# Attention and two gated MLPs on one core: more places for loaded rows, full-height factor matmuls, and a last chunk finished block by block

## The chip, the cores and the metric

One core of one Trainium2 chip runs the whole program. The metric is the device time of one execution in microseconds. Times of the kernel before are from three timed runs, and one more execution was taken by the profiler.

## The reference

```python
# attention: 4 batches, 8 heads, 576 positions, head width 64; scale = 1/8
scores = scale * q @ k.T                                   # causal
cum    = cumsum(max(s, 0))
scores = where(causal, -1e9, scores + min(-(cum_i - cum_j), 0))
attn   = softmax(scores);  x = attn @ v                    # as 2304 tokens x 512
# layer 1: RMS norm, then a gated MLP, 512 -> 1536 -> 512
xn = x / sqrt(mean(x*x) + 1e-6) * rms_g
x1 = (silu(xn @ w_gate) * (xn @ w_val)) @ w_out
# layer 2: the same without the norm
y  = (silu(x1 @ w2_gate) * (x1 @ w2_val)) @ w2_out
```

## The kernel before

Every large product is made of three float32r matmuls: an operand is split into a rounded part (H) and its rest (L), and H*H, H*L and L*H are summed. ACT rounds, DVE or POOL subtracts to get the rest. The engines' instruction order is written by a planner at build time: `Plan.op` records each operation with a cost in ns, what it reads and writes, and a priority; `Plan.run` lists them engine by engine, always the ready one of smallest priority number. A changed cost, buffer or dependency can therefore move any instruction behind it. The SP queue, which issues nearly all DMAs, runs in order: a load whose buffer is not yet free holds back everything behind it.

The program has five stretches. **Attention with the first layer's gate and value products** (0 to 442 us): the heads of one batch are worked on while the matmuls of the batch before (`gate_value`, L1116) fill TensorE's free places. After each batch `normalise` makes the norm's factors: per token and head one number, which a transpose brings into the first 16 partitions of a tile (`rT`, L1089); a matmul with the constant matrix `sel` (L1096) spreads these 16 rows over 128 partitions, four such matmuls a batch, and the result scales x. `sel` has 16 partitions, so this matmul uses 16 of TensorE's 128 rows. `rT` lies in the place of xH's last quarter, which is overwritten with rounded x afterwards. **The rest of those products** (442 to 506). **The first output stage** (506 to 626): two passes of `strassen_out`, each of seven products of a block with 512 tokens (Strassen's scheme), and a `plain_out` over the last 256 tokens. **Layer 2's gate and value products** (626 to about 896), which store rows to DRAM. **The second output stage** (from about 896): the same two kinds of passes, then the stores of the result.

In an output stage a row of the hidden layer (128 x 512, or x 256 in `plain_out`) comes in by `fetch_row`: a load by SP into a place of ring "h" (L1453), the rounding by ACT into ring "H" (L1395), the rest by DVE into ring "L" (L1398). A row serves six matmuls of `strassen_out` (L1478), or twelve of `plain_out` (L1533). Each of the three rings has four places, used in turn: a load waits until the row four back has been subtracted from, and a rounding until TensorE is through with the row four back. At a product's end ACT copies the two banks out (`keep`, L1488) or DVE adds them (`add`, L1494). `sums_of_rows` (L1178 loads, L1183, L1186 stores) prepares sums of rows for the second pass beside the first pass, on the same SP queue and on DVE.

At the very end, `plain_out` goes through the twelve rows, and within a row through the four output blocks (dd). `store_rest` copies each block out in two halves, 128 columns by DVE with a store on SP, 128 by ACT with a store on ACT's queue.

Of the kernel before, what the change touches and what calls it, by code (L numbers as in the profile page):

```python
# [333 lines left out]
def tile_kernel(  # L334
# [80 lines left out]
    sel = buf("m1", "sel", [2 * NH, 2 * KD, D], F32R)  # L415
# [106 lines left out]
    def setup():  # L522
# [17 lines left out]
        for x in (xs, xL[0], *xH):  # L540
            op(NONE, 0, lambda en, x=x: x.bufs[0](), w=[])
        op(ACT, 450, lambda en: en.dma_start(out=cum(), in_=s), w=[cum], pri=-3e6, later=2000)
# [37 lines left out]
        def later():  # L580
            def selectors(en):
                for j in range(2):
                    en.memset(half()[64 * j:64 * j + 64, j:j + 1], 1.0)
                    en.memset(half()[64 * j:64 * j + 64, 1 - j:2 - j], 0.0)
                en.memset(f32(zsel()), 0.0)
                for j in range(2):
                    en.memset(f32(zsel()[64 * j:64 * j + 64, 2 * KD - 2 + j:2 * KD - 1 + j]), 1.0)
                en.tensor_tensor(
                    out=sel()[:],
# [5 lines left out]
            op([(POOL, 1800), (DVE, 1200)], 0, selectors, r=[ident, "early 1"], w=[half, zsel, sel], pri=5.5)  # L595
# [367 lines left out]
    def normalise(H, L, g, tot, pri, split=True):  # L963
# [93 lines left out]
        def rT():  # L1057
            return H(KD - 1, lo, n)[:2 * NH]
# [30 lines left out]
        op(ACT, c_act(n), lambda en: en.activation(rT(), tp()[:2 * NH, skip:skip + n], ACTF.Copy),  # L1089
           r=[tp], w=last, pri=pri)  # L1090
        banks = (ps, mo_bank())
        for k in range(KD):
# [3 lines left out]
            op(PE, (c_mm(n) + 90, 2 * NH), lambda en, rs=rs, k=k: en.matmul(  # L1096
# [427 lines left out]
    def plain_out(row, WO, ring, acc, tiles, pri, scale=1.0, store=None):  # L1524

        n = 256
        for f in range(KF):
            H, L = fetch_row(ring, *row(f), n, pri + f)
            for dd in range(KD):
                name = "A11 A21 A12 A22".split()[dd // 2 + 2 * (f // K6)]  # L1530
                for i, (z, xx) in enumerate(((0, H), (0, L), (1, H))):
                    part, w = weight(WO, name, f % K6, dd % 2, z)
                    op(PE, c_mm(n), lambda en, dd=dd, w=w, xx=xx, f=f, i=i: en.matmul(  # L1533
                        acc[dd]()[:, :n], w(), xx(), start=f == 0 and i == 0,
                        stop=f == KF - 1 and i == 2), r=[part, xx],
                       w=[acc[dd]] if f or dd or i else acc, pri=pri + f)
# [216 lines left out]
    extra = {z: two(free_w[i], F32 if z == "h" else F32R, "h" + z) for i, z in enumerate("hHL")}  # L1753
# [180 lines left out]
```

## Time and profile before

| what | us |
|---|---|
| median of 3 runs | 1046.23 |
| lowest and highest | 1043.33, 1046.81 |
| profiled execution, its own time | 1044.21 |
| its span, first to last instruction | 1042.4 |
| PE busy | 1031.7 (99%) |
| DVE, ACT, POOL busy | 769.5 (74%), 633.9 (61%), 261.2 (25%) |
| DMA | 212.07 MB, mean 203 GB/s |

PE is TensorE's matmuls, DVE is VectorE, ACT is ScalarE, POOL is GpSimd; "SPq" and "ACTq" are the queues that issue DMAs. Matmuls are pipelined and overlap in the records, so the time that one takes is the distance from its start to the next start, not its recorded duration, and a PE that shows as busy can still be slower than its best. The granted clock is TensorE's, as a share of 2.4 GHz; 1.00 is the upper of its two levels.

### The profile page before, as it was taken

To read this page: it belongs to the slowest core of one execution; us is meant where nothing else is said; L and a number is where in the kernel's file an instruction comes from. 1 tells how busy PE (TensorE), PEld (TensorE's weight loads), DVE (VectorE), ACT (ScalarE), POOL (GpSimd) and SP (SyncE) were. 2 spreads that over 40 slices of the span, in tenths; PEclk is the share of its full clock that TensorE was granted. 3 is DMA by queue.
4 is the path that set the end of the run, shared out by engine and by line. 5 is a ranking of instruction groups with operands and counts; after the bars stand their busy time and mean duration, and the time that the engine had idled before them with its cause. 6 is when DMAs were issued, how large, how long until landed. Compare 5 with 4: busy or idle time off the path is not lost.

```text
span 1042.4 us, 17573 instructions
## 1 busy us (share of the span) xinstructions
PE 1031.7 (99%) x5546; PEld 901.1 (86%) x5546; DVE 769.5 (74%) x1751; ACT 633.9 (61%) x1318; POOL 261.2 (25%) x351
## 2 busy tenths in 40 slices
PE   9999999999999999999999999999999999999998
PEld 9988888998999899899887889888888888878888
DVE  7989877778778787568878987766668667876562
ACT  6889877766676465234466866455665455665652
POOL 3668744443333240100000000211222221300000
PEclk9999999999999999999999999999999999999999
DMA  9874533433345674378887662676676767888673
GB/s 326 267 244 136 185 123 110 132 116 121 99 138 151 220 241 155 124 236 264 279 282 250 199 207 96 223 236 207 213 239 220 249 239 245 281 273 252 217 241 99
DMA packets 123293, 212.07 MB, mean 203 GB/s; under 512 B 19072, under 2 KB 47488, under 8 KB 123200
## 3 DMA queue, kind: packets, MB, share of 16 engines
q1 hardware_dynamic: 122576, 210.61, 62.3%
q8 instruction: 44, 0.72, 0.3%
q10 hardware_dynamic: 624, 0.34, 0.1%
q14 instruction: 49, 0.40, 0.1%
HBM read 146.33 MB, written 64.56 MB: 202 GB/s over the span
## 4 chain that ended last, share of the span: by engine, by line
PE 88%; DMA 5%; DVE 3%; ACT 2%; issue 1%; SPq 0%; POOL 0%; ACTq 0%; DVEq 0%; POOLq 0%
PE mo L1116 24%; PE mo L1649 11%; PE sps L1649 9%; PE mo L1478 7%; PE tp L1478 6%; PE tp L787 5%; PE sps L1478 4%; PE tp L775 3%; PE sps L705 3%; PE mo L1725 3%; PE mo L1533 2%; PE tp L1649 1%; PE sps L1116 1%; PE tp L1116 1%; DMA h_d<-t 1%; PE sps L830 1%
## 5 line engine op out<-in xcount | busy, mean ns | idle before, releaser
L1398 DVE TENSOR_TENSOR hL<-hh,hH 128x512 fp32r<-128x512 f32 (+1 forms) x192 | 126.5, 667 | 70.4 <-ACT hH L1395 69.5
L1116 PE MATMUL mo<-xH,L 128*128 128x448 f32 (+2 forms) x472 | 171.8, 364 | 0.2 <-DVE L L488 0.2
L1116 PE MATMUL mo<-xL,H 128*128 128x448 f32 (+2 forms) x472 | 170.9, 362 | 0.6 <-DVE xL L1105 0.6
L1116 PE MATMUL mo<-xH,H 128*128 128x448 f32 (+2 forms) x472 | 170.5, 362 | 0.0
L1395 ACT ACTIVATE hH<-hh 128x512 fp32r<-128x512 f32 (+1 forms) x192 | 114.9, 603 | 89.8 <-DVE hL L1398 21.3
L1478 PE MATMUL mo<-hH,wo 128*128 128x512 f32 x312 | 98.3, 390 | 0.4 <-ACT hH L1395 0.4
L1116 PEld LDWEIGHTS mo<-xL,H 128*128 128x128 f32 x472 | 88.8, 188 | 8.2 <-issue 1.2
L1116 PEld LDWEIGHTS mo<-xH,L 128*128 128x128 f32 x472 | 88.8, 188 | 7.8 <-issue 1.2
L1116 PEld LDWEIGHTS mo<-xH,H 128*128 128x128 f32 x472 | 88.8, 188 | 6.2 <-issue 0.2
L742 ACT ACTIVATE sc<-sc,col 128x256 f32<-128x256 f32 (+2 forms) x96 | 60.6, 631 | 48.0 <-DVE col L731 47.6
L1478 PEld LDWEIGHTS mo<-hH,wo 128*128 128x128 f32 x312 | 58.6, 188 | 13.2 <-ACT hH L1395 1.2
L780 DVE TENSOR_TENSOR pTB<-tp,pTB 128x512 fp32r<-128x512 f32 (+1 forms) x96 | 56.3, 596 | 12.4 <-ACT pTB L778 11.9
L1655 ACT ACTIVATE u<-sps 128x512 f32<-128x512 f32 x48 | 28.6, 595 | 55.0 <-PE sps L1649 53.1
L1478 PE MATMUL mo<-hL,wo 128*128 128x512 f32 x156 | 61.3, 393 | 0.7 <-DVE hL L1398 0.4
L1478 PE MATMUL tp<-hH,wo 128*128 128x512 f32 x192 | 60.4, 389 | 0.0
L778 ACT ACTIVATE pTB<-tp 128x512 fp32r<-128x512 f32 (+1 forms) x96 | 48.8, 519 | 18.5 <-PE tp L775 17.7
L787 PEld LDWEIGHTS tp<-pTB,vst 128*128 128x128 f32 x320 | 52.9, 188 | 4.0 <-DVE pTB L780 0.3
L787 PE MATMUL tp<-pTB,vst 128*128 128x448 f32 (+3 forms) x320 | 55.3, 314 | 0.0
L1478 PE MATMUL sps<-hH,wo 128*128 128x512 f32 x168 | 53.2, 390 | 0.2 <-ACT hH L1395 0.2
L775 PE MATMUL tp<-ident,sc 128*128 128x128 f32 x320 | 51.3, 273 | 1.4 <-ACT sc L742 1.3
L719 POOL TENSOR_SCALAR_AFFINE_SELECT sc<-cb 128x128 f32<-128x128 f32 x96 | 34.6, 375 | 54.8 <-PE tp L775 48.0
L1664 ACT ACTIVATE u<-u 128x512 f32<-128x512 f32 x48 | 29.7, 631 | 30.0 <-DVE u L1659 29.9
(291 smaller groups left out, 2783.1 us busy)
## 6 DMA issues: line engine op xcount, KB each, us to landing
raw<-in_w_gv SPq DMA_DIRECT2D x44, 511.8 KB, 5.8
tb<-h_d SPq DMA_DIRECT2D x48, 256.0 KB, 3.6
t<-tb SPq DMA_DIRECT2D x48, 256.0 KB, 2.6
hh<-t SPq DMA_DIRECT2D x48, 256.0 KB, 3.3
lq<-in_qk SPq DMA_DIRECT2D x32, 288.0 KB, 4.0
cb<-cum_d SPq DMA_DIRECT2D x32, 288.0 KB, 3.6
hh<-h_d SPq DMA_DIRECT2D x36, 256.0 KB, 3.6
row0B<-u SPq DMA_DIRECT2D x24, 256.0 KB, 3.5
```

What stands on the lines that cost most here:

```text
L705: op(PE, c_mm(n), lambda en, pt=pt, at=at, c=c, n=n, z=z, kk=kk: en.matmul(pt()[:, :n], qst[j]()[:, at:at + 128], kk()[:, c:c + n], start= ...
L719: op(POOL, 165 + 0.85 * m, lambda en: en.affine_select(out=sc()[:m, o:o + m], in_=cb()[:m, o:o + m], pattern=[[-1, m]], base=0, compare_op ...
L742: op(ACT, c_act(o + m, 2) + 35, lambda en: en.activation(sc()[:m, :o + m], sc()[:m, :o + m], ACTF.Exp, scale=-1.0, bias=col()[:m, 0, t:t + 1],
L775: op(PE, C_TR, lambda en, pt=pt, a=a, kb=kb, t=t: en.transpose(pt()[:, a * P:a * P + P], self.sc[t]()[:, kb * P:kb * P + P], ident()), r=[ ...
L778: op(ACT, c_act(n), lambda en, pt=pt, c=c: en.activation(place(H, c), source(pt, c), ACTF.Copy), r=[pt], w=[(H, c)], pri=pri)
L780: op(DVE, c_tt(n), lambda en, pt=pt, c=c: en.tensor_tensor(out=place(L, c), in0=source(pt, c), in1=f32(place(H, c)), op=ALU.subtract), r=[ ...
L787: op(PE, c_mm(n), lambda en, w=w, z=z, kb=kb, d0=d0, n=n, o=o: en.matmul(po()[:, o:o + n], vst[j]()[:, kb, :], pT[z]()[:, d0:d0 + n], star ...
L1116: op(PE, c_mm(n), lambda en, a=a, x=x, c=c, k=k, i=i: en.matmul(ps()[:, :n], a()[:, c], x(k, lo, n), start=(k == 0 and i == 0), stop=(k == ...
L1395: op(ACT, c_act(n) + 35, lambda en: en.activation(H(), src(), ACTF.Copy), r=[src, *after], w=[H], pri=pri)
L1398: lambda en: en.tensor_tensor(out=L(), in0=src(), in1=f32(H()), op=ALU.subtract),
L1478: op(PE, c_mm(n), lambda en, m=m, w=w, xx=xx, kk=kk, i=i: en.matmul(ps[m]()[:, :n], w(), xx(), start=first and kk == 0 and i == 0, stop=kk ...
L1649: op(PE, c_mm(n), lambda en, w=w, xx=xx, cut=cut, kk=kk, i=i: en.matmul(ps()[:, :n], W[w]()[:, cut], xx(), start=first and kk == 0 and i == 0,
```

## The change

Three things. `sel` gets 128 partitions, zero below the first 16, and the factor matmul reads all 128 rows of `rT`'s place; for that the last quarter of both xH buffers is set to zero once at the start, and the set-up of the constants waits for DVE's `cumulate` by an instruction that reads its result. In both output stages ring "h" gets six places, rings "H" and "L" three. The last `plain_out` goes through its last two rows block by block, and `store_rest` copies each block out whole, in turn by DVE (with SP's queue) and ACT (with its own).

```diff
-    sel = buf("m1", "sel", [2 * NH, 2 * KD, D], F32R)
+    sel = buf("m1", "sel", [P, 2 * KD, D], F32R)
...
+        for x, n in zip(xH, (512, NQ)):
+            op([(POOL, 520), (DVE, 400)], 0, lambda en, x=x, n=n: en.memset(
+                f32(x(KD - 1, 0, n)), 0.0), w=x.keys(KD - 1, ALL), pri=4.5)
...
             def selectors(en):
+                en.tensor_scalar(out=fenced()[:, 1:2], in0=f32(cumHL()[:, :1]), scalar1=1.0,
+                                 scalar2=1.0, op0=ALU.mult, op1=ALU.mult)
...
+                en.memset(f32(sel()), 0.0)
                 en.tensor_tensor(
-                    out=sel()[:],
+                    out=sel()[:2 * NH],
...
-            op([(POOL, 1800), (DVE, 1200)], 0, selectors, r=[ident, "early 1"], w=[half, zsel, sel], pri=5.5)
+            op([(POOL, 2300), (DVE, 1500)], 0, selectors, r=[ident, cumHL, "early 1"],
+               w=[half, zsel, sel], pri=5.5)
...
         def rT():
-            return H(KD - 1, lo, n)[:2 * NH]
+            return H(KD - 1, lo, n)
...
-            op(PE, (c_mm(n) + 90, 2 * NH), lambda en, rs=rs, k=k: en.matmul(
+            op(PE, c_mm(n) + 90 * (not split), lambda en, rs=rs, k=k: en.matmul(
                 rs(), sel()[:, 2 * k:2 * k + 2].rearrange("p h d -> p (h d)"),
                 rT(),
                 start=True, stop=True), r=[sel, *last], w=[rs], pri=pri)
...
-    def plain_out(row, WO, ring, acc, tiles, pri, scale=1.0, store=None):
+    def plain_out(row, WO, ring, acc, tiles, pri, scale=1.0, store=None, tail=0):
...
+        ends = []
         for f in range(KF):
             H, L = fetch_row(ring, *row(f), n, pri + f)
+            if f >= KF - tail:
+                ends.append((f, H, L))
+                continue
             for dd in range(KD):
...
+                products(dd, f, H, L, pri + f)
+        for dd in range(KD):
+            for end in ends:
+                products(dd, *end, pri + KF + dd)
...
+    extra = [two(free_w[i], F32R if i == 2 else F32, "hr"[i == 2]) for i in range(3)]
...
+            + single(f"h{z}1", F32 if z == "h" else F32R, "h" + z) for z in "hHL"}
+    ring["h"] += extra[0] + extra[1]
+    ring["H"].append(extra[2][0])
+    ring["L"].append(extra[2][1])
...
+    last_r = two(free_w[20], F32R, "hr")
+    ring = {"h": [x for t in ("hh0", "hh1", "tmp0", "tmp1") for x in single(t, F32, "hh")]
+            + two(free_w[19], F32, "hh"),
+            "H": [x for t in ("hH0", "hH1") for x in single(t, F32R, "hH")] + last_r[:1],
+            "L": [x for t in ("hL0", "hL1") for x in single(t, F32R, "hL")] + last_r[1:]}
...
     def store_rest(xo, ps, dd):
-        for z, e in enumerate((DVE, ACT)):
...
+        if dd % 2:
+            op(ACT, c_act(256), lambda en: en.activation(xo(), ps()[:, :256], ACTF.Copy), r=[ps],
+               w=[xo], pri=-1.0e4)
+        else:
+            op(DVE, c_tt(256), lambda en: en.tensor_copy(xo(), ps()[:, :256]), r=[ps], w=[xo],
+               pri=-1.0e4)
+        op((SP, ACT)[dd % 2], (4 * P * 256, 450)[dd % 2], lambda en: en.dma_start(
+            out=outT[dd * P:(dd + 1) * P, 2048:2304], in_=xo()),
+           r=[xo], w=[("out4", dd)], pri=-1.0e4)
```

Three places show how the written order moves. First SP's queue, in the middle of the first pass of `strassen_out`: `hh` and `h` are places of the ring of loaded rows, `h_d` and `t` rows and sums of rows in DRAM, `tb` the buffers of `sums_of_rows`. The kernel before:

```order
L1186 DMA t_85<-tb 128x512
L1453 DMA hh<-t_83 128x512 x4
L1186 DMA t_87<-tb 128x512
L1453 DMA hh<-t_83 128x512
L1186 DMA t_86<-tb 128x512
L1453 DMA hh<-t_83 128x512
L1186 DMA t_88<-tb 128x512
L1453 DMA hh<-h_d_70 128x512 x6
```

and the changed one at the same place:

```order
L1461 DMA hh<-t_83 128x512 x2
L1194 DMA t_85<-tb 128x512
L1461 DMA h<-t_83 128x512 x4
L1194 DMA t_87<-tb 128x512
L1461 DMA hh<-h_d_70 128x512
L1194 DMA t_86<-tb 128x512
L1461 DMA hh<-h_d_70 128x512
L1461 DMA h<-h_d_70 128x512 x4
L1194 DMA t_88<-tb 128x512
```

The loads stand further ahead of the stores of the sums: before, the six loads of `h_d_70` come behind all four stores, now the first comes ahead of the third store and the other five ahead of the fourth.

Second ACT's order at the start of the same pass, where `hH` and `r` are places of the ring of rounded rows and `x` the copies of a finished product (`keep`). Before:

```order
L1395 ACTIVATE hH<-hh 128x512 x5
L1488 ACTIVATE x_6396<-sps_6326 128x512
L1488 ACTIVATE x_6396<-sps_6332 128x512
L1395 ACTIVATE hH<-hh 128x512 x6
L1488 ACTIVATE x_6396<-tp_6401 128x512
L1488 ACTIVATE x_6396<-tp_6408 128x512
```

and in the changed kernel:

```order
L1403 ACTIVATE r<-h 128x512
L1403 ACTIVATE wo<-ov 128x512
...
L1403 ACTIVATE hH<-h 128x512 x2
L1403 ACTIVATE r<-h 128x512
L1403 ACTIVATE hH<-hh 128x512 x2
L1496 ACTIVATE x_6399<-sps_6329 128x512
L1496 ACTIVATE x_6399<-sps_6335 128x512
L1403 ACTIVATE r<-h 128x512
L1403 ACTIVATE hH<-h 128x512 x2
```

Before the first pair of copies nine rows are rounded in the kernel before (four of them further up) and eight in the changed one (three further up), so that the rounding runs three rows ahead of a product's end before, and two now; between two pairs of copies there are six roundings in both.

Third the end of PE's queue, where `mo0` to `mo3` are the banks of the four output blocks, `hH`, `hL` the parts of a row, and `hr` the third place, which holds both parts. Before, the last row (each line of two other such lines for the rest left out):

```order
L1533 MATMUL mo0_10632<-hH_9697,wo_9807 128x256
L1533 MATMUL mo0_10632<-hL_9705,wo_9807 128x256
...
L1533 MATMUL mo2_10638<-hH_9697,wo_9807 128x256
...
L1533 MATMUL mo1_10643<-hH_9697,wo_9773 128x256
...
L1533 MATMUL mo3_10648<-hH_9697,wo_9773 128x256
```

and in the changed kernel the last two rows:

```order
L1540 MATMUL mo2_10635<-hr_9700,wo_9810 128x256 x3
L1540 MATMUL mo0_10641<-hH_8848,wo_9810 128x256
...
L1540 MATMUL mo0_10641<-hr_9700,wo_9810 128x256 x3
...
L1540 MATMUL mo3_10646<-hr_9700,wo_9775 128x256 x3
...
L1540 MATMUL mo1_10651<-hr_9700,wo_9775 128x256 x3
```

Before, a block gets its last three matmuls three apart, all within the last twelve; now a block is finished with six matmuls in a row, and the four blocks end six matmuls apart.

## Rows read from the trace of the kernel before

**Rows 1.** Windows by stage: busy us (x instructions) by engine, granted clock, DMA share.

```profile
60.00:442.00 382.00, 380.41 (x2192) 341.43 (x2190) 296.39 (x906) 257.70 (x607) 164.38 (x244) 1.00 0.47 149
...
506.00:575.00 69.00, 67.43 (x290) 53.68 (x289) 53.15 (x87) 42.08 (x73) 1.58 (x1) 1.00 0.84 267
575.00:626.00 51.00, 51.00 (x233) 42.28 (x232) 45.92 (x78) 36.87 (x68) 1.30 (x1) 1.00 0.66 205
```

**Rows 2.** One line, L1096, the factor matmuls: durations in ns, first and last start.

```profile
L1096 PE MATMUL mo<-xH,sel x24: 275/462/470, 30.7 to 441.6; 16*128 16x448 f32 x16, 16*128 16x256 f32 x8
```

**Rows 3.** Timeline, PE, around one factor matmul: start us, us, instruction.

```profile
339.85 0.37 PE L1116 MATMUL mo<-xH,H 128*128 128x448 f32 x1
340.05 0.37 PE L1116 MATMUL mo<-xL,H 128*128 128x448 f32 x1
340.35 0.46 PE L1096 MATMUL mo<-xH,sel 16*128 16x448 f32 x1
340.74 0.47 PE L1116 MATMUL mo<-xH,L 128*128 128x448 f32 x1
341.05 0.37 PE L1116 MATMUL mo<-xH,H 128*128 128x448 f32 x1
```

**Rows 4.** Timeline, PE, around two factor matmuls in a row.

```profile
336.94 0.37 PE L1116 MATMUL mo<-xH,H 128*128 128x448 f32 x1
337.23 0.67 PE L1096 MATMUL mo<-xH,sel 16*128 16x448 f32 x2
337.84 0.47 PE L1116 MATMUL mo<-xL,H 128*128 128x448 f32 x1
```

**Rows 5.** Chain that ended last, first output stage: start us, us, what.

```profile
506.10 8.18 PE sps L1478 x36
...
565.07 5.25 DMA hh<-h_d
...
575.09 8.18 PE tp L1478 x36
```

**Rows 6.** Timeline, ACT, two idle stretches of that stage.

```profile
546.42 1.94 ACT L1395 ACTIVATE hH<-hh 128x512 fp32r<-128x512 f32 x3 [1.96 <-DMA hh<-h_d]
...
557.21 0.63 ACT L1395 ACTIVATE xHB<-x 128x512 fp32r<-128x512 f32 x1 [2.76 <-DVE x L1494]
```

**Rows 7.** Timeline, ACT, then DVE, at the end of one product.

```profile
513.69 1.22 ACT L1488 ACTIVATE x<-sps 128x512 f32<-128x512 f32 x2
...
515.46 0.69 DVE L1398 TENSOR_TENSOR hL<-hh,hH 128x512 fp32r<-128x512 f32 x1 [0.55 <-ACT hH L1395]
...
518.31 0.68 DVE L1183 TENSOR_TENSOR tb<-tb 128x512 f32<-128x512 f32 x1
```

**Rows 8.** Timeline, PE, start of the second output stage.

```profile
919.09 0.83 PE L1478 MATMUL mo<-hH,wo 128*128 128x512 f32 x2
920.15 0.50 PE L1478 MATMUL mo<-hL,wo 128*128 128x512 f32 x1 [0.23 <-DVE hL L1398]
```

**Rows 9.** Timeline, all engines, end of the program.

```profile
1037.48 1.37 DVE L1865 COPY oo<-mo 128x128 f32<-128x128 f32 x4 [3.81 <-PE mo L1533]
...
1038.24 0.28 PE L1533 MATMUL mo<-hH,wo 128*128 128x256 f32 x1
...
1040.04 0.34 ACTq L1868 DMA_DIRECT2D out_dram<-oo  x1
```

**Rows 10.** DMA issues of the last 27 us: KB each, median us to landing.

```profile
hh<-rest_d SPq DMA_DIRECT2D x11, 128.0 KB, 2.1
...
out_dram<-oo ACTq DMA_DIRECT2D x4, 64.0 KB, 1.7
```

**Rows 11.** DMA issues, whole program: stores of 128 KB.

```profile
h_d<-t SPq DMA_DIRECT2D x22, 128.0 KB, 3.4
```

**Rows 12.** One line, L959, a copy of 256 columns by ACT.

```profile
L959 ACT ACTIVATE x<-mo x5: 383/383/384, 16.8 to 36.1; 128x256 f32<-128x256 f32 x5
```

**Rows 13.** Timeline, POOL, first instruction after the set-up.

```profile
20.79 0.81 POOL L485 TENSOR_SCALAR H<-raw 128x512 fp32r<-128x512 f32 x1 [14.99 <-DVE raw L479]
```

More of the change, by code (lines that the diff above doesn't have):

```diff
@@ L1088, in normalise @@
                r=[rr, ident], w=[tp], pri=pri)
-        op(ACT, c_act(n), lambda en: en.activation(rT(), tp()[:2 * NH, skip:skip + n], ACTF.Copy),
+        op(ACT, c_act(n), lambda en: en.activation(rT()[:2 * NH], tp()[:2 * NH, skip:skip + n],
+                                                   ACTF.Copy),
            r=[tp], w=last, pri=pri)
@@ L1522, in strassen_out, with products @@
         done(p5, 1, 0)
-    def plain_out(row, WO, ring, acc, tiles, pri, scale=1.0, store=None):
+    def plain_out(row, WO, ring, acc, tiles, pri, scale=1.0, store=None, tail=0):
         n = 256
+        def products(dd, f, H, L, at):
+            name = "A11 A21 A12 A22".split()[dd // 2 + 2 * (f // K6)]
+            for i, (z, xx) in enumerate(((0, H), (0, L), (1, H))):
+                part, w = weight(WO, name, f % K6, dd % 2, z)
+                op(PE, c_mm(n), lambda en, w=w, xx=xx, i=i: en.matmul(
+                    acc[dd]()[:, :n], w(), xx(), start=f == 0 and i == 0,
+                    stop=f == KF - 1 and i == 2), r=[part, xx],
+                   w=[acc[dd]] if f or dd or i else acc, pri=at)
+        ends = []
         for f in range(KF):
             H, L = fetch_row(ring, *row(f), n, pri + f)
+            if f >= KF - tail:
+                ends.append((f, H, L))
+                continue
             for dd in range(KD):
[L1530 to L1536, printed above, removed]
+                products(dd, f, H, L, pri + f)
+        for dd in range(KD):
+            for end in ends:
+                products(dd, *end, pri + KF + dd)
         for dd in range(KD):
@@ L1751, in rows1 @@
         return row
-    extra = {z: two(free_w[i], F32 if z == "h" else F32R, "h" + z) for i, z in enumerate("hHL")}
+    extra = [two(free_w[i], F32R if i == 2 else F32, "hr"[i == 2]) for i in range(3)]
     ring = {z: single(f"h{z}0", F32 if z == "h" else F32R, "h" + z)
-            + single(f"h{z}1", F32 if z == "h" else F32R, "h" + z) + extra[z] for z in "hHL"}
+            + single(f"h{z}1", F32 if z == "h" else F32R, "h" + z) for z in "hHL"}
+    ring["h"] += extra[0] + extra[1]
+    ring["H"].append(extra[2][0])
+    ring["L"].append(extra[2][1])
     WO1 = {}
@@ L1831, in tile_kernel @@
                            P3 + 40 * (KF - 1) - 30 + 10 * i if i else P3 + 40 * (K6 + 2))
-    ring = {"h": [x for t in ("hh0", "hh1", "tmp0", "tmp1") for x in single(t, F32, "hh")],
-            "H": [x for t in ("hH0", "hH1") for x in single(t, F32R, "hH")]
-            + two(free_w[19], F32R, "hH"),
-            "L": [x for t in ("hL0", "hL1") for x in single(t, F32R, "hL")]
-            + two(free_w[20], F32R, "hL")}
+    last_r = two(free_w[20], F32R, "hr")
[3 more added lines that the diff above has]
+            "L": [x for t in ("hL0", "hL1") for x in single(t, F32R, "hL")] + last_r[1:]}
     def store_out(p):
```

12 lines of the change are left out of this document (2 added, 10 removed).

## The prediction

> **What bounds the kernel now.** I read the stages first. From 60 to 442 us PE is busy for 380.41 of 382 us, and the granted clock is 1.00, the upper of its two levels, as in every stage shown; from 506 to 575 us PE is busy for 67.43 of 69 us and the DMA engines for 0.84 [rows 1]. So TensorE is the bound nearly everywhere, and a gain must take time away from PE itself or close one of its few gaps. Since busy matmuls overlap, I then looked at distances between starts, and found PE slow without being idle in two places, beside a tail in which it is done and the program is not.
>
> The first place is the factor matmul. Ordinary matmuls of 448 columns start 0.20 us apart. Around one factor matmul, of 16 rows, the three distances from 340.05 to 341.05 are 0.30, 0.39 and 0.31, that is 1.00 where 0.60 is due [rows 3]: the matmul itself and both its neighbours lose, 0.40 us a visit. Two in a row cost the same once: 0.90 for three distances from 336.94 to 337.84, 0.30 too long, and the one behind them is long as in the single visit, 0.11 [rows 4]. The slow distance is no wait that ends late: the matmul behind the factor matmul is an ordinary one, with its operands long there, and it too is late.
>
> The second place is the first output stage. An undisturbed product of 36 matmuls takes 8.18 us, 0.227 a matmul. From 506.10 to 575.09 eight products take 68.99 us where 65.4 are due: 3.5 us lost [rows 5]. The chain leaves PE there for the load of a row, 5.25 us from issue to landing at 565.07 [rows 5]; ACT stood idle for 1.96 us until 546.42 for such a load, but for 2.76 us until 557.21 for an addition by DVE that stood ahead in its order [rows 6]. In the second output stage the like happens once: 1.06 us from 919.09 to 920.15 for two distances that take 0.45, 0.6 lost [rows 8].
>
> The tail: PE's last matmul starts at 1038.24, ACT issues the last store at 1040.04, and the span ends at 1042.4 [rows 9].
>
> **Factor matmuls over 128 rows.** There are 24, 16 of 448 columns and 8 of 256, between 30.7 and 441.6 us [rows 2]. In PE's timeline the 16 stand as ten single ones and three pairs, the 8 as four pairs. With all rows in use their shape is that of the matmuls around them, so I take their own distance, 0.20, as the price after. Thirteen visits by 0.40 give 5.2 us, all in the stretch in which PE is never idle, so all of it on the path. The four visits before 51 us lie where PE waits for others now and then: at most 1.6 us, at least nothing, and I take 0.8. Sum 6.0, between 5.2 and 6.8 if the shape is the cause.
>
> The Trainium skill has a rule that speaks against this: "TensorE: Matmul & The Clock Gate", section "Why this matters for your kernels", says "K=32 single mm = same time as K=128", so that fewer rows make a matmul neither faster nor slower. By that rule the edit would save nothing and the sum would be 2.8 us; by the rows it saves 6.0. The trace differs from it here [rows 3], and it stands among the rivals.
>
> The new set-up costs nothing that I can find on the path. POOL stands idle for 14.99 us until 20.79 [rows 13], after the constants' set-up; that set-up now waits for DVE's `cumulate` and has two clearings more, of 448 and of 512 columns. Neither can cost more than the 0.81 us of the 512-column conversion in the same row, so 1.6 us and the wait fit into the cover; without it, they would delay the first conversions on POOL one for one. DVE clears one buffer among its first operations; bounds 0 and 0.7 us (a 512-column operation on DVE takes 0.69 [rows 7]), and I take 0, since PE waits there for loads.
>
> **Six places for loaded rows, three for rounded ones.** No operation is added. Of the 3.5 + 0.6 = 4.1 us lost in the output stages, those with a load at their root go if the load is issued two rows (2.7 us) earlier, since 2.7 is more than the 1.96 that ACT waited; the loads now stand ahead of stores of sums that they stood behind. The stall with an addition at its root is no matter of places. I take half, 2.1 us. The upper bound is 4.1. The lower bound comes from the other edit: rounding now runs two rows ahead of a product's end and not three. At the end of the first product, at 514.28, ACT's two copies start at 513.69, the next rounding follows, and its rest ends at 515.46 + 0.69 = 516.15 [rows 7]. With three places this row is the third of the next product, needed 12 matmuls after 514.28, at 517.0: 0.85 us to spare. One sum of 0.68 us by DVE (as at 518.31 [rows 7]) in between fits; two do not, and cost 0.5. In the stretch 575 to 626 DVE is busy for 45.92 of 51 us [rows 1], so this can happen: I put the lower bound at four such boundaries, a loss of 2.0.
>
> **The tail.** Before, DVE's first copy starts at 1037.48, when the first block's last matmul, nine of 0.12 before 1038.24, started at 1037.16: 0.32 later [rows 9]. Now the fourth block ends last again, at the same time, the other three 6, 12 and 18 matmuls (0.72 us each) earlier, so copies and stores no longer queue: each engine has one copy and one issue per 1.44 us. The last copy starts at 1038.24 + 0.32 = 1038.56, takes 0.38 on ACT for 256 columns [rows 12], and the store is issued at about 1038.96 in place of 1040.04. It is of 128 KB; 64 KB took 1.7 us to land there, loads of 128 KB took 2.1 in the same stretch [rows 10], stores of 128 KB 3.4 over the whole program [rows 11]. With 2.1, as the nearest, the gain is 1.08 - 0.4 = 0.7; with 1.7 it is 1.1, with 3.4 a loss of 0.6. The two last rows must be rounded some 1.1 us earlier than now, which the idle ACT and DVE cover (three places leave the last row 0.36 + 1.44 us for a rounding and a rest of 0.4 each).
>
> **The planner.** The order changes in PE's queue from the first full batch on, with the same operations. PE never lacks work there, so I take 0; for the range I allow 1.5 either way, the size of the gap that PE has in 382 us [rows 1].
>
> **Sum.** 6.0 + 2.1 + 0.7 = 8.8 us from the profiled execution's 1044.21 gives 1035.4. That execution lies 2.0 under the median of the runs, 1046.23, and inside their spread; I add half of this and predict 1036.5. About 0.3%, 3.1 us, is what a measurement of this kernel can tell from no change: faster means under 1043.1, slower over 1049.4.
>
> **Rivals.**
> - *The rings give nothing, or take up to 2 us.* The DMA share of 0.84 [rows 1] speaks for it: loads issued earlier then only queue longer. Against it speaks that the stalls are single ones, with products of 8.18 us under the same traffic between them. 1045.2 - 6.7 = 1038.5, up to 1040.5, with other costs 1042.
> - *The factor matmuls stay slow.* If the loss hung on their place in the stream (a fresh bank, an operand that ACT has just written) and not on 16 rows, the edit would change nothing: 1045.2 - 2.8 = 1042.4. Against it speaks that the neighbours lose as well [rows 3], and that two in a row pay once [rows 4]. This is also the time by the Trainium skill's rule above.
> - *Slower: two rows of lead are too few.* Place: the product ends in the output stages, 2 stages by 2 passes by 7 = 28. Price: 0.5 us wherever two DVE operations come ahead of the third row's rest. All 28 would cost 14 us and give 1038.5 + 14 = 1052.5; the gain is used up at 14 of them, and over 1049.4 it takes 22. For it speaks DVE's load in 575 to 626 [rows 1]; against it that the rest has the smaller priority number than the sums, so the planner puts it first.
>
> **How the numbers follow.** Forecast 0.60, its own range 1033 to 1039.5; rings without gain 0.22, 1038.5 to 1042 and in a quarter of it beyond; factor matmuls unchanged 0.08, near 1042.4; too little lead 0.10, 1045 to 1053. The range 1032 to 1042.5 holds the first, most of the second and half of the third: 8 in 10. Faster: 0.60 + 0.16 + 0.02 = 0.78; same: 0.06 + 0.06 + 0.01 = 0.13; slower 0.09.
>
> **What would show it.** Right: the factor matmuls read 128 rows, and PE's starts around them stay 0.20 apart; the stretch of gate and value products ends 5 to 6 us earlier; ACT's idle time for loaded rows in the first output stage goes, and eight products take 65.5 to 67.5 us; the last store is issued 0.7 us after PE's last start. Wrong: distances of 0.3 to 0.4 remain; or ACT and DVE stand waiting for PE at every product's end and PE then for the rest; or the last store takes over 3 us to land. A new idle stretch of PE in attention, from the new order, would make the prediction wrong from outside its steps.

## The result, and the profile after

The changed kernel takes 1035.86 us (median of six runs, 1035.16 to 1037.15), the kernel before 1044.77 beside it (six runs, 1042.60 to 1046.81): 0.9916 of it, with an interval of 0.9898 to 0.9933. Two more sets of runs, below, gave 0.9915 and 0.9927. In this set of runs the medians differ by 8.9 us where 8.8 were forecast, and the median lies within 0.7 us of the forecast 1036.5. The sum came out right; its terms did not all, and the experiments are needed to see it.

The two profiled executions lie 8.6 us apart (spans 1042.4 and 1033.8). Lines have moved: L1096 is now L1104, L1116 is L1124, L1395 is L1403, L1398 is L1406, L1478 is L1486, L1488 is L1496, L1533 is L1540. First the windows by stage of the changed kernel (stretch, its length, then busy us of PE, PEld, DVE, ACT and POOL, granted clock, DMA share, GB/s), against [rows 1]:

```profile
60.00:436.00 376.00, 375.54 (x2188) 342.23 (x2189) 294.45 (x905) 255.86 (x606) 170.95 (x248) 1.00 0.48 149
...
500.00:569.00 69.00, 69.00 (x306) 57.13 (x305) 58.16 (x94) 46.85 (x80) 1.29 (x1) 1.00 0.86 282
569.00:620.00 51.00, 50.64 (x238) 41.87 (x237) 46.26 (x78) 36.09 (x66) 1.30 (x1) 1.00 0.61 188
```

In the first output stage PE is busy for all of the 69 us (67.43 before) and gets 306 matmuls done in them, 16 more. Then PE's timeline around two single factor matmuls, against [rows 3]:

```profile
335.83 0.36 PE L1124 MATMUL mo<-xH,L 128*128 128x448 f32 x1
336.03 0.37 PE L1104 MATMUL mo<-xH,sel 128*128 128x448 f32 x1
336.24 0.36 PE L1124 MATMUL mo<-xH,H 128*128 128x448 f32 x1
336.44 0.36 PE L1124 MATMUL mo<-xL,H 128*128 128x448 f32 x1
```

All distances are 0.20 or 0.21: the matmul and both neighbours have lost their excess. The chain that ended last, in the first output stage, against [rows 5]:

```profile
500.13 8.18 PE sps L1486 x36
...
565.43 8.16 PE tp L1486 x36
...
589.03 6.20 DMA raw<-in_w_gv
595.23 0.02 issue
595.25 0.80 ACT cvy L1325
...
596.69 0.69 DVE r L1406
597.38 0.04 issue
597.42 1.43 PE mo L1486 x5
```

Eight products take 565.43 - 500.13 = 65.30 us where they took 68.99, and no load of a row is in the chain any more. One wait is new, at 597.42 in the second pass, though not in every execution (the changed kernel's second profile, below, doesn't have it): a load of layer 2's weights takes 6.20 us, its conversion by ACT stands ahead of a row's rounding in ACT's order, and PE loses 0.6 us on that row's rest. The groups of ACT's instructions in these 69 us say the same as the chain (count, busy us and mean ns, then idle us before them with what ended it); first the kernel before:

```profile
L1395 ACT ACTIVATE hH<-hh 128x512 fp32r<-128x512 f32 x46 | 29.0, 630 | 23.4 <-DMA hh<-h_d 7.8 <-DMA hh<-t 6.4 <-PE sps L1478 4.9
```

and the changed kernel, whose roundings stand in three groups:

```profile
L1403 ACT ACTIVATE hH<-h 128x512 fp32r<-128x512 f32 x18 | 11.3, 629 | 4.9 <-DVE hL L1406 2.2 <-PE sps L1486 1.5 <-PE mo L1486 0.7
L1403 ACT ACTIVATE hH<-hh 128x512 fp32r<-128x512 f32 x16 | 10.1, 632 | 9.7 <-DVE hL L1406 4.4 <-DVE r L1406 3.6 <-PE sps L1486 0.7
L1403 ACT ACTIVATE r<-h 128x512 fp32r<-128x512 f32 x16 | 10.1, 630 | 6.2 <-DVE hL L1406 2.2 <-PE sps L1486 1.5 <-PE mo L1486 1.4
```

ACT waited 7.8 + 6.4 = 14.2 us for loaded rows before and does not now. It waits for places of its own ring: between product ends its roundings start 1.36 us apart (519.23, 520.59, 521.95), the time in which PE goes through one row, and this costs PE nothing here. The second output stage starts with two waits of PE, against one in [rows 8]; PE's timeline:

```profile
905.08 1.45 PE L1486 MATMUL mo<-hr,wo 128*128 128x512 f32 x5 [0.74 <-DVE hr L1406]
...
915.12 0.50 PE L1486 MATMUL mo<-hL,wo 128*128 128x512 f32 x1 [0.18 <-DVE hL L1406]
```

And the end of the program, all engines, against [rows 9]:

```profile
1029.90 0.42 DVE L1886 COPY oo<-mo 128x256 f32<-128x256 f32 x1 [1.01 <-PE mo L1540]
...
1030.06 0.52 PE L1540 MATMUL mo<-hr,wo 128*128 128x256 f32 x3
1030.62 0.38 ACT L1883 ACTIVATE oo<-mo 128x256 f32<-128x256 f32 x1 [1.05 <-PE mo L1540]
1031.03 0.34 ACTq L1888 DMA_DIRECT2D out_dram<-oo  x1
```

PE's last matmul starts at 1030.06 + 2 x 0.12 = 1030.30; the last store is issued 0.73 later, and the span ends 3.5 later, at 1033.8. Before, these were 1.80 and 4.2.

### The profile page after: what moved, and what is told of

Same layout as the page of the kernel before. It is cut to its first block, busy times and chain, and to the rows that moved or that the text cites. A ratio compares the mean times of both kernels' runs of the same rounds, so it can differ in the third digit from the quotient of the medians.

```text
span 1033.8 us, 17596 instructions
## 1 busy us (share of the span) xinstructions
PE 1024.6 (99%) x5546; PEld 901.6 (87%) x5546; DVE 765.8 (74%) x1748; ACT 631.8 (61%) x1315; POOL 264.5 (26%) x357
## 4 chain that ended last, share of the span: by engine, by line
PE 90%; DMA 4%; DVE 3%; issue 1%; ACT 1%; SPq 0%; POOL 0%; POOLq 0%; DVEq 0%; ACTq 0%
PE mo L1124 24%; PE mo L1667 11%; PE sps L1667 9%; PE mo L1486 8%; PE sps L1486 6%; PE tp L1486 6%; PE tp L794 5%; PE tp L782 3%; PE sps L712 3%; PE mo L1743 3%; PE mo L1540 2%; PE tp L1667 1%; PE tp L1124 1%; PE sps L1124 1%; PE sps L837 1%
## 5 line engine op out<-in xcount | busy, mean ns | idle before, releaser
L1124 PE MATMUL mo<-xH,L 128*128 128x448 f32 (+2 forms) x472 | 171.3, 363 | 0.2 <-DVE L L488 0.2
L1124 PE MATMUL mo<-xL,H 128*128 128x448 f32 (+2 forms) x472 | 170.2, 361 | 0.7 <-DVE xL L1113 0.7
L1124 PE MATMUL mo<-xH,H 128*128 128x448 f32 (+2 forms) x472 | 170.5, 362 | 0.0
L1124 PEld LDWEIGHTS mo<-xL,H 128*128 128x128 f32 x472 | 88.8, 188 | 7.2 <-DVE xL L1113 0.9
L1124 PEld LDWEIGHTS mo<-xH,L 128*128 128x128 f32 x472 | 88.8, 188 | 6.8 <-DVE L L488 0.4
L1124 PEld LDWEIGHTS mo<-xH,H 128*128 128x128 f32 x472 | 88.8, 188 | 5.6
L1406 DVE TENSOR_TENSOR hL<-hh,hH 128x512 fp32r<-128x512 f32 (+1 forms) x96 | 63.8, 668 | 39.9 <-ACT hH L1403 39.2
L1403 ACT ACTIVATE hH<-hh 128x512 fp32r<-128x512 f32 (+1 forms) x96 | 57.6, 603 | 51.1 <-DVE hL L1406 21.1
L1486 PE MATMUL mo<-hH,wo 128*128 128x512 f32 x208 | 68.5, 389 | 0.0
L787 DVE TENSOR_TENSOR pTB<-tp,pTB 128x512 fp32r<-128x512 f32 (+1 forms) x96 | 56.3, 597 | 14.2 <-ACT pTB L785 13.5
L1630 POOL TENSOR_TENSOR tmp<-x,x 128x512 f32<-128x512 f32 x2 | 2.6, 1297 | 173.6 <-DVE x L1502 116.9
L1486 PEld LDWEIGHTS mo<-hH,wo 128*128 128x128 f32 x208 | 39.0, 188 | 8.1
L1131 ACT ACTIVATE t<-mo 128x448 f32<-128x448 f32 (+2 forms) x59 | 30.4, 515 | 24.8 <-PE mo L1124 18.7
L782 PEld LDWEIGHTS tp<-ident,sc 128*128 128x128 f32 x320 | 39.7, 140 | 6.1 <-DVE pTB L787 0.2
L1133 DVE SCALAR_TENSOR_TENSOR t<-t,mo 128x448 f32<-128x448 f32 (+2 forms) x59 | 34.8, 591 | 13.7 <-ACT t L1131 13.5
```

The lines of the kernel that those rows point to most:

```text
L782: op(PE, C_TR, lambda en, pt=pt, a=a, kb=kb, t=t: en.transpose(pt()[:, a * P:a * P + P], self.sc[t]()[:, kb * P:kb * P + P], ident()), r=[ ...
L787: op(DVE, c_tt(n), lambda en, pt=pt, c=c: en.tensor_tensor(out=place(L, c), in0=source(pt, c), in1=f32(place(H, c)), op=ALU.subtract), r=[ ...
L1124: op(PE, c_mm(n), lambda en, a=a, x=x, c=c, k=k, i=i: en.matmul(ps()[:, :n], a()[:, c], x(k, lo, n), start=(k == 0 and i == 0), stop=(k == ...
L1133: op(DVE, c_tt(n), lambda en: en.scalar_tensor_tensor(out=t()[:, :n], in0=t()[:, :n], scalar=1.0, in1=gp()[:, :n], op0=ALU.add, op1=ALU.mu ...
L1403: op(ACT, c_act(n) + 35, lambda en: en.activation(H(), src(), ACTF.Copy), r=[src, *after], w=[H], pri=pri)
L1406: lambda en: en.tensor_tensor(out=L(), in0=src(), in1=f32(H()), op=ALU.subtract),
```

## The experiments

Each was run beside the kernel before; ratios are to it. The kernel before had medians of 1042.98, 1044.06 and 1043.34 us in the three groups of runs, so absolute times are compared only within a group (16 rows, 64 rows, old rings, old end; then rows alone, whole first part, the changed kernel again and the kernel before again; then lead alone, second stage, old cost and the changed kernel beside them).

**Is it the 16 rows?** The changed kernel, its order untouched, with fewer rows in the factor matmul:

```diff
-                rs(), sel()[:, 2 * k:2 * k + 2].rearrange("p h d -> p (h d)"),
-                rT(),
+                rs(), sel()[:16, 2 * k:2 * k + 2].rearrange("p h d -> p (h d)"),
+                rT()[:16],
```

> The changed kernel with the factor matmul over 16 rows again (its operands cut to the first 16 partitions), every other instruction and the whole order as in the changed kernel. Theory (a matmul of 16 rows among matmuls of 128 costs 0.40 us a visit, its neighbours included): 5.2 to 6.8 us more than the changed kernel's 1035.9, that is 1041.1 to 1042.7, with distances of 0.3, 0.4, 0.3 around the factor matmuls in PE's timeline. Rival (the loss hangs on a fresh bank, on an operand that ACT has just written, or was taken away by the new order): 1035.9 and distances of 0.20.

Measured: 1038.49 us, 0.9965 (0.9949 to 0.9981). PE's timeline around a factor matmul:

```profile
337.21 0.36 PE L1124 MATMUL mo<-xH,L 128*128 128x448 f32 x1
337.51 0.46 PE L1104 MATMUL mo<-xH,sel 16*128 16x448 f32 x1
337.90 0.47 PE L1124 MATMUL mo<-xH,H 128*128 128x448 f32 x1
338.21 0.36 PE L1124 MATMUL mo<-xL,H 128*128 128x448 f32 x1
```

0.30, 0.39 and 0.31 are back in the same place of the same stream, so the rows are the cause, and the rival (a fresh bank, an operand just written) is out. But the loss of time is less than the theory's. In the same group ran the changed kernel with the old end alone, 1036.38 us, of which the end is 0.6 (below); so 16 rows cost 1038.49 - 1035.74 = 2.75 us and not 5.2. The ratios, of different groups, would give 0.0038 to 0.0050, 4 to 5 us, with intervals of nearly 2 us either way on each; the table below decides, and gives 2.7.

With 64 rows (the edit is shown against the last one):

```diff
-                rs(), sel()[:16, 2 * k:2 * k + 2].rearrange("p h d -> p (h d)"),
-                rT()[:16],
+                rs(), sel()[:64, 2 * k:2 * k + 2].rearrange("p h d -> p (h d)"),
+                rT()[:64],
```

> The same with 64 rows in place of 16. Theory A (a matmul that leaves rows out costs, however many it leaves out, because TensorE changes over before and after it): as with 16 rows, 1041.1 to 1042.7, and the distances of 0.3, 0.4, 0.3 are there. Theory B (the cost follows the share of idle rows, 64 of 128 against 112 of 128): some 3.4 us, 1039.3, and distances about half as long again as due. Theory C (only a matmul of very few rows costs): 1035.9.

Measured: 1039.13 us, 0.9963 (0.9949 to 0.9978), not to be told from 16 rows, and PE's timeline is the same:

```profile
338.60 0.37 PE L1124 MATMUL mo<-xH,L 128*128 128x448 f32 x1
338.90 0.46 PE L1104 MATMUL mo<-xH,sel 64*128 64x448 f32 x1
339.29 0.47 PE L1124 MATMUL mo<-xH,H 128*128 128x448 f32 x1
339.60 0.36 PE L1124 MATMUL mo<-xL,H 128*128 128x448 f32 x1
```

Theory A holds at these two counts: 16 rows or 64, the visit costs the same 0.39 us, so the price does not follow the number of idle rows.

**Where the other microseconds are.** The kernel before with 128 rows alone, its set-up as in the changed kernel and the planner's cost left as it was, by which PE's order stays that of the kernel before to the row:

```diff
-    sel = buf("m1", "sel", [2 * NH, 2 * KD, D], F32R)
+    sel = buf("m1", "sel", [P, 2 * KD, D], F32R)
...
-            return H(KD - 1, lo, n)[:2 * NH]
+            return H(KD - 1, lo, n)
```

> The kernel before with the factor matmul over 128 rows alone: its set-up as in the changed kernel, but the planner's cost for it left as it was, so that PE's order is that of the kernel before to the row. Theory (0.39 us for each of 13 visits from 150 us on, and at most 1.6 for the four before): 5.1 to 6.7 us less than the kernel before, 0.9935 to 0.9951 of it; all distances around the factor matmuls 0.20. Rival (rows cost less than that, and most of the 6.0 us was the new order and one late store): 3 to 4 us, 0.996 to 0.997.

and the same with the changed kernel's cost as well, which is the whole first part:

```diff
-            op(PE, (c_mm(n) + 90, 2 * NH), lambda en, rs=rs, k=k: en.matmul(
+            op(PE, c_mm(n) + 90 * (not split), lambda en, rs=rs, k=k: en.matmul(
```

> The whole first part of the change on the kernel before: as the last, and the planner's lower cost, by which attention's order becomes that of the changed kernel. Theory (a visit costs nothing once all rows are used, so that it no longer matters that the new order has ten visits in place of thirteen): as the last within 0.5 us. Rival (the new order is worth 1 us or more by itself): 1 to 1.5 us less than the last.

Measured: 1039.52 us, 0.9954 (0.9938 to 0.9969), for the rows alone, and 1038.83 us, 0.9955 (0.9941 to 0.9969), for the whole part; by time the two can't be told apart. Beside them ran the changed kernel, and one more profile of the kernel before:

> The changed kernel once more, beside the next three on the same chip. Theory (attention's time differs from one execution to the next by how late stores of h_d land in the first 75 us, by up to 2 or 3 us): median within 1 us of 1035.9, the first output stage starts at 500.0 give or take 1.5, all stages behind it as long as in the first profile within 0.3. Rival (a profile repeats itself to 0.3 us): starts at 500.0 give or take 0.3.

> The kernel before, profiled once more. Theory (its wait of PE at 71 us, 1.5 us, behind ACT, which waited 1.9 us for the landing of a store of h_d, belongs to that one execution): the wait is gone, or a like one stands at another place before 75 us, and the first output stage starts at 504.5 in place of 505.9, give or take 1. Rival (it belongs to the order of the kernel before): it is there again at 71 us, and the changed kernel gained these 1.5 us by its order.

Measured: 1035.15 us, 0.9915 (0.9901 to 0.9929); and an execution of 1046.06 us. The question is answered by two instructions that all these kernels have, the first `kHH,qst` matmul at 60 us and the first matmul of the output stage. PE's timeline of the kernel before, second profile:

```profile
60.66 0.47 PE L830 MATMUL sps<-kHH,qst 128*128 128x448 f32 x1 [0.20 <-DVE col L731]
...
504.71 0.40 PE L1478 MATMUL sps<-hH,wo 128*128 128x512 f32 x1
```

with 128 rows in the old order:

```profile
60.17 0.47 PE L837 MATMUL sps<-kHH,qst 128*128 128x448 f32 x1 [0.20 <-DVE col L738]
...
499.11 0.40 PE L1485 MATMUL sps<-hH,wo 128*128 128x512 f32 x1
```

with 16 rows in the new order:

```profile
59.51 0.47 PE L837 MATMUL sps<-kHH,qst 128*128 128x448 f32 x1 [0.20 <-DVE col L738]
...
502.25 0.39 PE L1486 MATMUL sps<-hH,wo 128*128 128x512 f32 x1
```

and the changed kernel's first profile:

```profile
60.19 0.47 PE L837 MATMUL sps<-kHH,qst 128*128 128x448 f32 x1 [0.20 <-DVE col L738]
...
499.97 0.39 PE L1486 MATMUL sps<-hH,wo 128*128 128x512 f32 x1
```

| from the first of these to the second, us | old order | new order |
|---|---|---|
| 16 rows | 444.05 (second profile before; first 445.42) | 442.74 |
| 64 rows | | 442.71 |
| 128 rows | 438.94; 438.73 (last experiment) | 439.78, 439.95, 440.09 (changed kernel, three profiles); 440.11 (first part alone) |

In the old order the rows give 444.05 - 438.94 = 5.1 us, which is 13 visits of 0.39. In the new order they give 442.74 - 440.0 = 2.7. With 16 rows the new order itself gains 1.3, since it has ten visits in this stretch, four single ones and six pairs; with 128 rows, when a visit costs nothing, it loses 1.1. Not all ten visits get their time back: the one at 430 us in the changed kernel has two matmuls that take 0.90 where 0.41 is due, for they now wait for DVE's `x`. That accounts for 0.4, and half of another visit, at 245 us, for 0.2; the remaining 0.6 of 3.9 - 2.7 I can't place.

The first profile before stands 1.4 us above the second. Its ACT and PE at 70 us:

```profile
70.12 0.38 ACT L1123 ACTIVATE t<-mo 128x256 f32<-128x256 f32 x1 [1.92 <-DMA h_d<-t]
```

```profile
71.15 0.55 PE L775 MATMUL tp<-ident,sc 128*128 128x128 f32 x3 [1.30 <-ACT sc L742]
```

and ACT in the second profile:

```profile
68.89 0.38 ACT L1123 ACTIVATE t<-mo 128x256 f32<-128x256 f32 x1 [0.55 <-DMA h_d<-t]
```

A store of `h_d` landed late in the one execution, ACT's next write to its buffer waited, and PE behind it. In the other ACT's wait is 0.55 and PE's is gone, with the same order: the theory stated ahead of that profile holds. The second and third profile of the changed kernel start the output stage at 499.45 and 501.39, not within 0.3 of 499.97. But one part of what was expected fell: the stages behind do not repeat to 0.3 us. From the first matmul of the output stage to PE's last one, the three profiles of the changed kernel take 530.3, 529.0 and 530.8 us, and the two of the kernel before 532.3 and 535.4.

**The rings.** The changed kernel with four places in all three rings:

```diff
-    extra = [two(free_w[i], F32R if i == 2 else F32, "hr"[i == 2]) for i in range(3)]
+    extra = {z: two(free_w[i], F32 if z == "h" else F32R, "h" + z) for i, z in enumerate("hHL")}
...
-            + two(free_w[19], F32, "hh"),
...
+            + two(free_w[19], F32R, "hH"),
...
+            + two(free_w[20], F32R, "hL")}
```

> The changed kernel with all three rings of both output stages at four places again. Theory (six loaded places remove the waits for a row's load; three rounded places cost a little elsewhere; net of both by the two profiles 2.0 us): 1037.0 to 1038.8, centre 1037.9; the first eight products of the first output stage take 68 to 69 us again instead of 65.3, the wait of 0.7 us for a third row's rest in the second pass goes, and the second output stage is as fast as now or up to 0.8 us faster. Rival (the rings gave nothing and the two profiles differ by the new order in attention): 1035.9 with eight products of about 65.4.

Measured: 1037.31 us, 0.9946 (0.9928 to 0.9963). In its group that is 1.6 us more than 1036.38 - 0.6 (old end alone); the ratio lies 0.0019 to 0.0031, 2 to 3 us, above those of the changed kernel, with intervals that overlap. Its profile doesn't show this loss where it was expected. Its eight products took 66.04 us, not 68 to 69, though ACT waited 12.8 us there for loaded rows; the wait at 597 us is gone, and the second output stage is 0.3 to 1.6 us shorter than in the changed kernel's profiles. From the first matmul of the output stage to PE's last it takes 529.2 us; its time went in attention, to a late store at 50 us (last section). This profile alone would leave the rival standing.

By the chains, eight products with four places took 68.99 and 70.34 (the kernel before), 71.31 (rows alone), 67.91 (first part) and 66.04 here, 68.9 in the mean. With six and three they took 65.30, 65.38 and 65.34 in the changed kernel's three profiles, 65.4 with 16 rows and with the old end, 65.9 with 64 rows, 65.8 in the run below with four places in the second stage alone, and 66.9 in the one with the old order (last experiment): 65.7 in the mean. So the rings give 3.2 us there in the mean; the fastest of the five is faster than the slowest of the eight. From the first matmul of the output stage to PE's last, five profiles with four places in both stages take 529.2 to 536.4 us, 533.2 in the mean, and seven with six and three 529.0 to 531.1, 530.4 in the mean. That is 2.8 us less, and most of the spread is gone. The groups are not alike, though: three of the five have the old order of attention (532.3 to 536.4), against one of the seven (531.1), and in the new order alone it is 532.6 and 529.2 against 529.0 to 530.8. How much of the 2.8 hangs on that order was not tried. The old rings do not always stall as in [rows 5].

Now the shorter ring of rounded rows without the longer one of loaded rows:

```diff
-    ring["h"] += extra[0] + extra[1]
+    ring["h"] += extra[0]
...
-            + two(free_w[19], F32, "hh"),
+            ,
```

> The changed kernel with four places for loaded rows in both output stages, and three for rounded ones as now: the shorter lead without the longer one. Theory (the gain is in the loads, and three rounded places cost nothing): as with four and four, 1.5 to 3 us over the changed kernel, all of it in waits of PE for a row's load or what hangs on it. Rival (three places cost 0.5 us at many product ends, and the six loaded ones pay for more than that): 4 us or more over the changed kernel, with PE waiting for the third row of products right behind a copy or an addition.

> The changed kernel once more, as the measure for the three beside it on the same chip: 1034.5 to 1036.5.

Measured: 1042.80 us, 0.9989 (0.9978 to 1.0001), against 1036.81 us, 0.9927 (0.9910 to 0.9944), for the changed kernel: 6.0 us more, and 0.0043, or 4.5 us, more than with four and four by the ratios, whose intervals do not overlap. So by time three rounded places are not free with four loaded ones, and my theory that they cost nothing fell. The rival's price is met, but its place only in part: the two longest distances between starts of PE in the eight products, 1.67 us at 555.30 and 0.96 at 538.47, stand at the second and the third row of a product. Eight products took 71.32, no more than in the slowest profile with four and four, so that the profile alone doesn't show the cost. The chain runs in circles through the loads:

```profile
510.63 4.27 DMA hh<-t
...
515.00 0.64 ACT hH L1403
...
515.66 0.70 DVE hL L1406
...
516.38 4.62 DMA hh<-t
...
521.11 0.64 ACT hH L1403
...
521.77 0.70 DVE hL L1406
...
522.49 3.81 DMA hh<-h_d
```

A load, its rounding and its rest take 5.75 us from 510.63 to 516.38, then 6.11, and only then can the same place be loaded again. With four places that is four rows in 5.75 to 6.11 us, while PE uses four rows in 24 x 0.227 = 5.44: at such rounds the ring can't keep up however early it starts, and a stock of rounded rows is used up until PE stands. Six places last for 36 x 0.227 = 8.17 us, longer than either round. This is the same with four and four (there too the chain goes from load to load: 516.95, 522.68 in the run with old rings, 5.73 apart), so it would explain what six places gain. It is an argument from these rounds, not a test: with six places the loads also stand further ahead of the stores of sums on SP's queue, and no run here separates the two. That three rounded rows are a smaller stock than four fits the 4.5 us, but no run separates it from the new order of ACT and DVE; six loaded places with four rounded ones were not run.

The second output stage by itself, with four places in all rings there and six and three in the first:

```diff
-    last_r = two(free_w[20], F32R, "hr")
...
-            + two(free_w[19], F32, "hh"),
-            "H": [x for t in ("hH0", "hH1") for x in single(t, F32R, "hH")] + last_r[:1],
-            "L": [x for t in ("hL0", "hL1") for x in single(t, F32R, "hL")] + last_r[1:]}
+            "H": [x for t in ("hH0", "hH1") for x in single(t, F32R, "hH")]
+            + two(free_w[19], F32R, "hH"),
+            "L": [x for t in ("hL0", "hL1") for x in single(t, F32R, "hL")]
+            + two(free_w[20], F32R, "hL")}
```

> The changed kernel with four places in all three rings of the second output stage alone. Theory (the rings give nothing there: PE's waits at its start hang on rows that have just been stored and on weights): within 0.4 us of the changed kernel. Rival A, as predicted: 0.6 us more, the wait for hL is back. Rival B (the third rounded place is what PE waits for at 905 us): 0.5 to 1 us less.

Measured: 1035.46 us, 0.9923 (0.9910 to 0.9937), against 1036.81 beside it; the intervals overlap. The windows of its start, first the changed kernel:

```profile
888.00:925.00 37.00, 35.79 (x154) 28.10 (x154) 27.50 (x42) 24.84 (x45) 4.22 (x4) 1.00 0.86 291
```

and with four places:

```profile
888.00:925.00 37.00, 36.72 (x165) 30.13 (x164) 29.38 (x43) 25.07 (x45) 5.97 (x4) 1.00 0.87 295
```

PE is idle for 0.9 us less there, and both of its waits, at 905 and 915 us, are gone. Of the 11 more matmuls five are short ones of 256 columns. The first wait, 0.39 to 0.75 us, stands in six of the seven profiles with six and three in this stage and in none of the six with four, of which four have the wait of [rows 8]. But from the stage's first matmul to PE's last, the seven take 136.5 to 138.5 us, 137.7 in the mean (the changed kernel's three 138.0, 136.9 and 138.1), and the six 136.3 to 138.1, 137.2 in the mean; the run here takes 136.3. So the rings give nothing there and cost some 0.5 us in the mean, inside the spread: rival B by the wait, unclear by time.

**The end.** The changed kernel with the old `plain_out` and `store_rest`:

```diff
-        if dd % 2:
...
+        for z, e in enumerate((DVE, ACT)):
+            c = slice(128 * z, 128 * z + 128)
...
-              [Part(xr, k, lambda t, k=k: t[:, k, :]) for k in range(KD)], P4 + 200, 1.0, store_rest,
-              2)
+              [Part(xr, k, lambda t, k=k: t[:, k, :]) for k in range(KD)], P4 + 200, 1.0, store_rest)
```

> The changed kernel with the old end: rows before blocks in the last two rows, each block copied out and stored in two halves. Theory: 0.6 to 0.7 us more, 1036.5, and the span ends 4.1 to 4.2 us after PE's last start instead of 3.5; nothing else in the program moves. Rival (larger stores land so much later that the end gains nothing): 1035.9 and 3.5 us.

Measured: 1036.38 us, 0.9940 (0.9924 to 0.9955). PE's last matmul starts at 1029.86, the last store is issued at 1031.66 and the span ends at 1034.0: 4.2 against 3.5. The time alone can't show 0.6 us; the profile does.

**The first part without its order.** The changed kernel with the planner's old cost:

```diff
-            op(PE, c_mm(n) + 90 * (not split), lambda en, rs=rs, k=k: en.matmul(
+            op(PE, (c_mm(n) + 90, 2 * NH), lambda en, rs=rs, k=k: en.matmul(
```

> The changed kernel with the planner's cost of the factor matmul as it was before, so that attention has the order of the kernel before, and the rest is the changed kernel's. Theory (with all rows in use the old order is 1.0 us faster between 90 us and the first output stage, since the new one has a wait of PE for DVE at 430 us and others): 0.7 to 1.2 us less than the changed kernel, 1034.3, and attention from 60 us to the first output stage takes 438.9 instead of 439.9. Rival (the order behind attention shifts too and takes it back): no difference, or more.

Measured: 1034.94 us, 0.9916 (0.9903 to 0.9930), the lowest median of its four, beside 1036.81. Attention from 60 us on takes 438.73, 1.2 less than in the changed kernel, as the theory has it. In the first output stage more than that comes back: eight products take 66.9 us in place of 65.3, 0.5 of it at 512 us as a wait for a row's rest. Whether the whole is faster stays open: the intervals overlap. With both old cost and old rings in the second output stage it was not tried.

## Why the prediction was right, point by point

**Factor matmuls: the mechanism right, the size too large.** Fewer than 128 rows was the cause, the neighbours do lose, and a visit costs 0.39 (0.40 said). Rival two, and with it the rule of the Trainium skill ("TensorE: Matmul & The Clock Gate", section "Why this matters for your kernels": "K=32 single mm = same time as K=128"), does not hold in the runs with 16 and 64 rows, where the matmul stands among others of 128 rows: it and its neighbours take 0.39 us more. A sentence on another page of the Trainium skill fits instead: "TensorEngine Tiling (Array Packing)", section "Tiling Modes", says that changing the tiling mode "drains the TensorE". If fewer rows count as another mode, it would make the price one per change of shape, whatever the rows: the two in a row [rows 4] and the 64 rows agree, while neither that they count as one nor that a drain is what happens is shown by any run here.

The step that was mis-sized is "thirteen visits by 0.40 give 5.2 us", together with "the planner: I take 0". For the old order the first is exact (5.1). But the changed kernel doesn't run in the old order; its new order takes back 1.1, so that the first part gives 4.0 us from 60 us on. The 0.8 for the early visits isn't to be seen, nor is a price of the new set-up: the instruction at 60 us starts at 60.52 and 60.66 before, and at 60.19, 59.50 and 61.30 in the changed kernel. That makes 4.0 to 4.3 in place of 6.0; by time the whole first part gave 0.0045 of 1044, 4.7 us. The first pair of profiles seems to confirm 6.0 to the digit, 506.10 - 500.13 = 5.97 in the chains, and does so by an accident: 1.4 us of it is the late store at 70 us.

**Rings: more than forecast where they were to help, less elsewhere.** The place was right: the waits of ACT for loaded rows are gone, and eight products take 65.3 (65.5 to 67.5 said). The step "I take half, 2.1 us" was too careful for the first stage (3.2 there in the mean of all profiles) and too hopeful for the second (some 0.5 lost in place of 0.3 gained). From the first output stage to PE's last matmul it makes 2.8 in the mean, near the 2.1 forecast. By time the rings gave 1.6 us in one group of runs and 3.0 in another (1038.83 - 1035.15 = 3.7, with the end's 0.6 taken off). The base of the forecast was lucky: the one profile behind it lost 3.5 us in the eight products, which is the mean of the five with the old rings, and these lose 0.6 to 5.9. The reason given, loads "two rows earlier", is weak: ACT waited 12.8 us for loads in the run with old rings, and PE lost only 0.6. That a place's round of 5.75 us and more is longer than four rows of PE's work and shorter than six fits better, but was not tested alone. The wait with an addition at its root, which I left out as "no matter of places", went too.

**Too little lead (the rival on the other side)** was underestimated as a mechanism: three rounded places with four loaded ones cost about 4.5 us by time. Whether six loaded places pay for this or take it away was not tried. It didn't show as 0.5 us at every product's end, and with six places it may show at the two or three waits named above.

**The end: right.** Forecast 0.7, measured 0.64: the issue came 0.73 after PE's last start (0.72 said), and the larger store took 0.4 longer to the end of the span, as the sum had it.

**The sum.** 4.2 + 2.8 + 0.6 = 7.6 by the parts of the profiles, against 8.9, 8.9 and 6.5 by the medians of three sets of runs (8.8, 8.9 and 7.6 by their ratios), of which the kernel before alone scatters by 4 us. The parts lie inside that scatter. The forecast of 8.8 came so close because a first term that was 1.8 too large stood beside a second that was 0.7 too small, and because the rest, 8.8 - 7.6 = 1.2 us, is less than these runs can tell; that is luck.

## What to carry to other kernels

Look at the distance between starts around each matmul that uses fewer rows than its neighbours: if it and both neighbours are late, fill the rows with zeros, which cost nothing here. Choose the places of a load ring by its round: load, conversion and release together should be shorter than the work that the places feed. A cut in the ring behind it was not free before that held here. When a change also moves a planner's order, run the operation alone in the old order; and before a profile is taken as the base of a ledger, take a second one.

## What the hardware showed that I had not expected

The cost of a matmul of few rows among full ones was the same at the two counts run: distances of 0.30, 0.39 and 0.31 us with 16 rows, and 0.30, 0.39 and 0.31 with 64.

After a short idle stretch PE's clock was lower, in two executions. In the run with old rings, ACT waited 5.24 us for the landing of one store:

```profile
51.40 0.39 ACT L1131 ACTIVATE t<-mo 128x256 f32<-128x256 f32 x1 [5.24 <-DMA h_d<-t]
```

PE stood behind it for 2.8 us, and the windows of that run show the granted clock (last but two):

```profile
50.20:52.20 2.00, 0.00 (x0) 0.00 (x0) 0.38 (x2) 0.80 (x2) 0.00 (x0) 0.88 0.94 295
...
53.00:54.00 1.00, 1.00 (x6) 0.93 (x6) 1.00 (x4) 1.00 (x3) 0.82 (x2) 0.50 0.95 365
...
57.00:58.00 1.00, 1.00 (x7) 1.00 (x6) 0.95 (x3) 1.00 (x4) 1.00 (x2) 0.50 1.01 405
...
60.00:64.00 4.00, 4.00 (x34) 3.97 (x33) 3.83 (x11) 2.94 (x6) 2.19 (x5) 1.00 0.39 122
```

From 53 to 58 us PE is busy all the time at 0.50, the lower of its two levels; so here the late store cost its wait and the slow microseconds behind it. The third profile of the changed kernel has the same after an idle stretch of 1.6 us, at 0.50 from 52 to 54 us; after the 1.30 us at 71 us in the kernel before the clock stayed at 1.00. ACT stands idle at about 48 us in the other twelve profiles too, for 2.0 to 3.3 us: the wait is there each time, and its length differs. Such waits, in the first 75 us, are one part of the 4 us by which runs of one kernel scatter here; that they are all of it was not tried.
